# The same steps of an attention and gated-convolution kernel in another order on all five engines

## Chip, cores and metric

The kernel runs on one core of one Trainium2 chip. The metric is the device time of one execution in microseconds; the time given is the median of the runs.

## What is computed

The reference is block-sparse attention (4 batches, 8 heads, 768 tokens, head size 64) followed by a gated convolution layer. Cut to what matters:

```python
scores = scale * q @ k.T                       # per batch and head, 768 x 768
mask = neighbours | first and last block | 3 random blocks per query block   # blocks of 32
attn = softmax(where(mask, scores, -1e9)); x = attn @ v     # heads side by side: 4 x 768 x 512
h = maximum(x @ w_in, 0)                       # 512 -> 1024
conv_out = sum over k of conv_w[k] * h shifted by k - 1     # 3 taps along the tokens
out = (h * sigmoid(conv_out)) @ w_out          # 1024 -> 512
```

## The kernel before

The kernel first builds a graph of some 1,800 steps in Python. A step is a short run of instructions of one kind (two matmuls, one activation, one transfer), with the steps it depends on, the engines that can do it and the buffers that it takes. Which step comes when is not decided in the program: a long string, `ORDER`, gives the whole order. `put_down` reads it from left to right, two characters for a step, one more for its engine where there are several to choose from, one more for each buffer that the step takes:

```python
o = ops[64 * CODE.index(line[x]) + CODE.index(line[x + 1])]
x += 2
engines = list(o.alts)
e = engines[0]
if len(engines) > 1:
    e = ENGINES[line[x]]
    x += 1
for b in o.allocs:
    b.index = CODE.index(line[x])
    x += 1
if o.fn is not None:
    o.fn(e)
```

Each engine works through its own steps in the order of the string and waits, where a step needs it, for steps of other engines. PE, ACT, DVE, POOL and SP are each one list in order; a transfer that waits holds up what stands behind it in the list of its engine.

The work by stages, with the names used later and their lines in the profile:

- The head: q and k of the first pair of heads are loaded by SP and ACT and cast (`cast_q`, `cast_k`, L327 and L331), transposed on PE (`k_tr` L460, `q_tr` L500 and L522) and copied into a slot `t` of rows 0 to 63 (`k_cp`, `q_cp`). Rows 64 to 87 of the slot hold the mask, which DVE makes from the sampled blocks (`a1` to `a5`, L271 to L299, tile `mtok`) and which `m_k`, `m_q0`, `m_q1`, `m_h1`, `m_r1` and `m_slot` copy into the slots. So a matmul over 88 rows gives scores and mask at once. PE runs `warm` and `fill` matmuls on a zero tile (L230) until real work is there.
- Later pairs of heads are loaded by POOL (L239: `ld_k`, `ld_q`, `ld_nq`, `ld_v`), held back by small `pace` copies on POOL (L407, L673). From the seventh pair on, k and q are transposed by transfers of SP (`xb`, L597, tile `stg`) and copied by DVE (`stg_cp`). Mask rows of these slots come by SP (`m_turn`, `m_last`). v is copied by `v_cp`.
- Attention: 144 units of 8 blocks of 128 x 128 scores. Per unit two `s` steps on PE (L762, tile `st`, two buffers), one `exp` on ACT (L774, tile `pt`, six buffers; the first unit has two), two `av` steps on PE (L799, tile `av`, two buffers). Four pairs of heads end in `rcp` and `norm` on DVE (L707, L709, tile `xtok`), and the result is transposed, by SP (`x_xb`, L718) or on PE (`x_tr` L728 and a copy `x_cp`), into tile `xT`.
- The layer behind it runs by segments of 384 tokens (the last one as 256 and 128), while the attention of the next segment goes on: `f1` on PE (L896, tile `mix`, two buffers shared with transposes and outputs), `relu` on ACT (L916) or DVE (L918) into `hE`, then on DVE `mul` (L954) and `add` (L962), `tanh` on ACT (L1001), `g1` and `g2` on DVE (L1004, L1009) into `gT`. The very last segment makes the taps as matmuls (`conv`, L973) and its tanh at L978. `f2` on PE (L831) multiplies by the second matrix, `ev` on ACT (L327) or DVE (L331) copies to `o2s`, and `out` on SP (L840) stores it.

The tile `mix` is held by one step at a time, so `f1` of the next part waits for the `relu` of the part two before it. The two `st` buffers let PE be two units of scores ahead of `exp`.

Of the kernel before, what the change touches and what calls it, by code (L numbers as in the profile page):

```python
# [25 lines left out]
6y36g2016h6B16C6D46l1RV1QV2wV36m16G06H6u1s1n6v6z5Y06I51p4X1w4Y2X14Z1x4+2Z14/2+501y511z5234222V5ZV21V6n26P16Q6R0
6A6E6F6U06V6J6K1j6o6L06M6p06W16S06Z16+6T6N16qV6OV1r6/2720732e02fV2gV743ih16X77178iiik07f07g794il1q7k17l7h51i
ijV002KV47m0in16Y707p07q7r1imViF0iGiHiI71ioipV17u17v7w2iJiq0ir7C075762z1isViK2AV42BV7D7H17I7E32C07a7b17i7j7niN1
7c17J42s17M07N2tV7o7s7t7x537R17S2DV2uV2EViO147y7O57z2iP7AiQiz1iLiR7T03007W07X7Y17diAit082183iBA2842iu870887F17G
ivV37K7L2N18938c18d7PiM07Q7U7V2OV02PViw07e1iS312/18h0ixiyV8i7Z7+0852Q17/0iV2iW8e48j58p18q3823j38r0868a8b8f8u08v  # L30
2SViT80iYiX8w18g8k8l8z18A2RV7BiC08s18B28E08FiD8G3iU8J18K8L4iEVj918R08S8tja8x8T58y8C8D8W18H8X8I36254378/090iZi+
j13jf0jg8Y09112YV0j28m18nj4j333V32Vi/941958M8N08U8V8Z8+92939c09d962j5j01mj63919h19ijh979e498jbj7j89j5ji158O29m0
9n9r19sjc818ojjA09o1jdA13ajo0jp9w09t29909a35V18P3f3g33cV3bV553i3d0562F057jl1jmjnA9x9E19FjqV3eV2jJ08Q23k09y3ju0
jv9f09g9J0jKjM9K9G0jLjwVjN9k9l9p3h3o2T13p19q9L49O19Pjr19u2G09T09U9v9z2HV2IV9Q5jO9B19Cjs9/1jx09A19V2jyjzAa0a139D
9b3r3s0jtVjR1jSjP3w1jUjA1jBa402U0jCA3l9Ha5a91aaa619I9M9NjD1jEae09Raf9Sab42VV2WVaj1jFAjZ2jTjVjQj+ag53u3tjWak9W9X
jG0a20jH9Y2k09Zj/al0jIAar0a3a7a8kv13Dacasadaw1axjXjYkj0ahat3ay1aB0aiamaCan1auavkk3E13G3Ak1k53k6k7k8k9k29+k3k4
aD4kaaG1aHao1azaAkwaI5aO0aEaFaPklkx3B23F3M3N0aQ2aT1aUaV0kbkckmknV23nVapaJkyaY0aZb11b2aK3v43xkzA33qV33zV3yVa+3
b31kE0kFkB1kCb60b7aR0aS3H0aL0be1kDV14kGAkZ0k+k/l0kK0kLbfaWb84kMAbg5kH1kIbj0kJV53I1bkkQ0l1bl2kRkSAbo1kT13P3Q23S
kAjekobpaXbt0a/bub0b4l2bq03mVaMl51l6bv3kN0kOb5kUl8kPV6ld2bB1bCb9ba1bb2bD1kVA7kW0bG0bHbhkXbI4bibmbnbL1brl73R3XbM
bcbsbwbxbQ0bRaq03T0jkaNkYAbN5bS2kd1bd3JbE0bFkebV1bWkp0lelfl9lall3c10l3lg3CV4lhkqbJbKkrl41by1lbbObPbX0c2c61lic33  # L40
3UkfkgkhA3bzlmljlolnlplcc7c813OV0bAkslqlk3LVbTbUlz1bYcb0ccbZ1c4cg1lrls3KV3VV13WVcd4ktA1b+0b/c5c9cachci5lAlBcelC
lDA2co0cpct1cfculI0lF1lGlHVlJlKVm10cjm2m4cq0cv3cy0czm3m5cD1ckcEcA4cF53+3/343403Y141kilt1lL0cr0cl2cmcI0lMlNAcscJ
lulO0lPcwcQ1cK2cR4c4d0m6lQVm91mam7mbmcm8cS1lvlwcxcV0cWcBcCcG3ZV1c+1c/cHlxA0cX3d04lR0cL42494hd30d4c01441cN1mdcO
d50lSlU1cM1lTAlVdb1dccTcUmelWVmh2mimfdg0lX0dhl+1mklYl/dd5lZVdl1cYcZdi2d1dmd2d6d7de0m0Adn1cnmjmgku4i0dq0drd80mp3
d9mrmlmqmsmx0ds3lE4e4fdv1mtdwmD1dfdx4mmmElycP45dD0dEdI1djdkdF5dodpdtdJdudymydN0dadz1dGdHdOmnmudK24q4r1dP1dA2mo
mFmzdBmvmwdS1dT46V247VdU3mAmBV34a24gd+0d/mGdLe31dMdQe4mHV1e04e52dC24jmY0e80mV1e9mWdRed1dVeemZdW4v4n4s4tea04E4F2
mXV08m+VdX1nh0njdY4w1ei0n21n3ejm/0n0ef5e10eq1ere2e6e7ebdZmI4o0ek14Jn1A94bV2ev0n50ecewes4ninkn4Anlegehex2np1el
em1eA1eBeC0en0nq4kV3eonsepn6etn7Aaeun81n9eF0eGeN1eOnaAnx2eyezeDnb0nceH5eS0eEeTeInrnt4lVeP1eJne1eX1eYeQ0eK2eL4u
4m4xnyndAbeU4eZ2nmnunznfnAmJ0mKeRngVnF3nGnB4pV3f00eVeMmLf1f51eWf6nvnnnHno0f25mP1mQmMfd0fef71mNA2ff4nCnInwnJ4yV4
mRe+e/fi1mSfjf34zVnDmTA0fn0f4o30o4fk2o5Ao61foo7fs1ftfp54G4Bo8Vot0ounEov4C14H4I4PnKnL4Q2fu3nN0nOf8f91fa1nMnT1ow  # L50
fA0fBnUfgnPfF1nVmC4K0484LoxfbfC04DA4fGfH1oyfhnQnRV1fK0nWflfLnZ0fmnXV3n+fc04RV0oz4MV04NVo01o1fP1fM4fQfU0fqfrfvfV
fwn/Ao2AfR2oAol1omfx0onfW5oofyopfD0oc0g01g1g23o91fEodg50oeAg6g70oqfInSoafJobVoB2oDoCof0ga1fNgbfOgc1fSoggf0ggoi1
fTfXfY1ojg3g4g8orohAgh4okAgn1gog9gs0gtoEfZ2osoX0oYgdmOnYfzf+oFoJ3oLgp2oKoMoGmU4A4Ogx1geoHgu5gygigjgq0oR1oSgrgv
gwf/gG0gHgk1oNoIgz3gloOgL1gMgI0gN1gAoToZgBoPoQoUo+gQ0gC0oVV1gDgRgZ1p71g+gS4g/2p8p9pah20h3h71o/V2h45pbV3gmpd0pe
pg1phpfV1cpiVh8hg0pm0pnh93poApB0pDpj1pkhhhl1gE0plAdgJ1gKgOgPhmgFA1hi0oWp0hn1pp1ps0gTgUpqh00h1h5pCpEhq0h6ptpFpG
prAehahbhrpuApJ1pKhs4gV2gWpLpMhz1hj1hc1pNhdhAgX1gYVpHpR2hkpOpv0pwhohe1hE0hFhphthuhfApxAfpy1pzpI1pSp10p2hB2hG5
pAAhv0pThwpPhC0hN1hOhP3p3hDhx1pUpQpVpWhyVhW0hHhJ2p4p5A0qk1hI1qlpZ3hKp+p/qmAghXqq0qrh/1hY0qsAhq0pXq1qB0qDq2qR1pY
q3qChQqh1hRq4qihL0i0i80i9hMA2hZ0h+q50q6i11i2q7q8qjAiia4i41hS0i5qn1i30ibqt2hTicquqSq9A1qwid2qEi60qoi7AqpAjqb0qc
ieqFhU1hVAqvqGqdif1qJ3igAqxpcqHqeqfA2ri1rjrkAqyqKqIqLqMqzr90rarbArA1qUqArf1rBrC0qNrgrhArc0rl0rmrdrn2qgqap6reAqO
qTrorprDqPqVqQrv1rwr31rq0r4rrrs2rtrurx3qWryrzrErL0rR1rF0r5rMrGrHrNrOqXqYrIrSrTrUr6rJA3rPA2rKrVVrWrQr7A1r8qZ0q+  # L60
# [997 lines left out]
```

## Time and profile before

| | us |
|---|---|
| Median of 3 runs (lowest, highest) | 207.86 (207.11, 208.13) |
| Span of the profiled execution | 205.4 |
| Its own time beside the span | not recorded apart from the runs; the median lies 2.46 above the span |
| Busy: PE, ACT, DVE, POOL | 197.1, 189.7, 184.9, 59.4 |
| Weight loads on PE | 142.3 |

A busy time is the union of an engine's records. Matmuls are pipelined and their records overlap, so a busy PE says less than the pace at which matmuls follow each other; both are used below. A row of the groups gives line, engine, operation, tiles, shape and count, then busy time and mean length in ns, then the engine's idle time ahead of these instructions and what ended it. A row of the timeline or of the chain gives start and length in us, engine, line and count. A row of the windows gives for each engine the busy time in that stretch and the number of instructions, then the granted clock, the share of the transfer engines and GB/s.

### The profile page before, as it was taken

The page shows a single profiled execution, that of the slowest core. Times are in us where ns is not written, and L with a number is a line of the kernel's source. Part 1 is how long each engine was busy: PE and PEld are TensorE (multiplying, and loading weights), DVE is VectorE, ACT ScalarE, POOL GpSimd, SP SyncE. Part 2 cuts the span into 40 slices and gives each one's busy share as a digit, 9 for nine tenths or more (in the row PEclk, how much of TensorE's full clock was granted, in tenths as well). Part 3 has the DMA queues.
Part 4 walks back from the last instruction along what each step waited for, and adds up shares of the span by engine and source line. Part 5 has one row for each costly group of instructions (what it writes and reads, how often), then busy time and mean ns, then how long its engine had stood idle before and what let it go on. Part 6 is the DMA issues. An engine that isn't in the chain of part 4 may idle for free.

```text
span 205.4 us, 6237 instructions
## 1 busy us (share of the span) xinstructions
PE 197.1 (96%) x2392; PEld 142.3 (69%) x2409; DVE 184.9 (90%) x572; ACT 189.7 (92%) x253; POOL 59.4 (29%) x113
## 2 busy tenths in 40 slices
...
GB/s 155 196 190 154 186 178 114 197 127 88 154 150 126 125 103 138 218 166 163 95 105 226 97 117 123 175 154 126 14 174 88 21 123 51 3 2 3 153 3 204
DMA packets 50969, 25.59 MB, mean 125 GB/s; under 512 B 36764, under 2 KB 47996, under 8 KB 50940
## 3 DMA queue, kind: packets, MB, share of 16 engines
...
q10 hardware_dynamic: 288, 0.30, 0.5%
q14 instruction: 10, 0.08, 0.1%
...
## 4 chain that ended last, share of the span: by engine, by line
PE 68%; ACT 15%; DVE 12%; issue 3%; ACTq 0%; DVEq 0%
PE st L762 22%; PE mix L896 15%; PE mix L831 15%; PE av L799 12%; ACT pt L774 11%; DVE m L954 3%; DVE t L331 2%; DVE m L962 2%; ACT m L1001 1%; DVE xtok L709 1%; PE st L831 1%; ACT vt L327 1%; DVE diag L379 1%; ACT hE L916 1%; PE mix L728 1%
## 5 line engine op out<-in xcount | busy, mean ns | idle before, releaser
L774 ACT ACTIVATE pt<-st 128x1024 bf16<-128x1024 f32 (+1 forms) x145 | 142.2, 1051 | 4.2 <-PE st L762 3.7
L762 PE MATMUL st<-t 88*128 88x256 bf16 (+2 forms) x600 | 90.5, 267 | 2.3 <-DVE t L331 1.2
L799 PEld LDWEIGHTS <-pt 128*128 128x128 bf16 x1152 | 54.0, 97 | 14.2
L762 PEld LDWEIGHTS <-t 88*128 88x128 bf16 x600 | 48.9, 97 | 21.0 <-issue 1.9
L799 PE MATMUL av<-vt,pt 128*128 128x65 bf16 x1152 | 60.5, 193 | 0.1
L896 PE MATMUL mix<-xT,winb 128*128 128x384 bf16 (+2 forms) x288 | 55.2, 307 | 0.1
L954 DVE TENSOR_SCALAR m<-hE,cw 128x382 bf16<-128x382 bf16 (+2 forms) x192 | 49.1, 312 | 0.4 <-ACT hE L916 0.2
L831 PE MATMUL mix<-woutb,gT 128*128 128x512 bf16 x167 | 47.2, 379 | 0.7
L962 DVE TENSOR_TENSOR m<-m 128x764 bf16<-128x764 bf16 (+2 forms) x64 | 34.1, 532 | 0.6
L896 PEld LDWEIGHTS <-winb 128*128 128x128 bf16 x288 | 24.0, 97 | 9.2 <-issue 0.6
L1001 ACT ACTIVATE m<-m 128x764 bf16<-128x764 bf16 (+2 forms) x32 | 27.1, 853 | 0.0
L831 PEld LDWEIGHTS <-gT 128*128 128x128 bf16 x200 | 17.1, 97 | 10.0 <-DVE gT L1009 1.2
L407 POOL COPY pace<-pt 1x1 bf16<-1x1 bf16 x24 | 6.4, 268 | 54.1 <-ACT pt L774 54.0
L916 ACT ACTIVATE hE<-mix 128x384 bf16<-128x384 f32 (+2 forms) x39 | 19.8, 519 | 0.4 <-PE mix L896 0.2
L1009 DVE TENSOR_TENSOR gT<-m,hE 128x764 bf16<-128x764 bf16 (+3 forms) x36 | 18.2, 509 | 0.4
L709 DVE TENSOR_TENSOR xtok<-av,rcp 128x384 bf16<-128x384 f32 (+2 forms) x36 | 18.3, 507 | 0.4
L239 POOL DMA_DIRECT2D nat<-in_q_dram x23 | 17.3, 752 | 3.8 <-DMA nat<-in_k_dram 1.6
L918 DVE TENSOR_SCALAR hE<-mix 128x384 bf16<-128x384 f32 x25 | 13.7, 553 | 4.3 <-PE mix L896 3.7
L331 DVE COPY t<-mix 64x384 bf16<-64x384 bf16 (+1 forms) x33 | 13.2, 411 | 0.6 <-PE mix L460 0.2
L239 POOL DMA_DIRECT2D nat<-in_k_dram x15 | 12.0, 803 | 3.0 <-issue 2.4
L1004 DVE TENSOR_SCALAR m<-m 128x764 bf16<-128x764 bf16 (+3 forms) x36 | 11.9, 334 | 0.7 <-ACT m L1001 0.7
L327 ACT COPY o2s<-mix 128x512 f32<-128x512 f32 x15 | 9.2, 613 | 3.3 <-PE mix L831 3.2
...
## 6 DMA issues: line engine op xcount, KB each, us to landing
...
```

The costliest lines, as they stand in the source:

```text
L239: return op(name, {eng: occ}, lambda e: on(e).dma_start(out=dst(), in_=src), prio, deps, dma=(kind, service), **kw)
L709: nm = op("norm", {"DVE": t_dps(128 * C)}, lambda e: nc.vector.tensor_tensor(out=xtok_t[xk.index][:, 0:C].rearrange("p c h d -> p h c d"), ...
L762: nc.tensor.matmul(out=st[:, 128 * x:128 * (x + n_)], lhsT=t[0:88, 12 + 6 * hh + kc, :], rhs=t[0:88, idx:idx + (n_ - 1) * (2 if P < NPE el ...
L774: nc.scalar.activation(out=pt_t[ptb.index][:, c0:c1], in_=st_t[stb.index][:, c0:c1], func=AF.Exp, bias=0.0, scale=0.125)
L799: nc.tensor.matmul(out=o[:, off:off + 65], lhsT=pt_t[ptb.index][:, 128 * x:128 * x + 128], rhs=V_t[vslot_b[P].index][:, hh, kc, 0:65], sta ...
L831: nc.tensor.matmul(out=acc(), lhsT=gT_t[gb.index][:, ffc, 128 * t:128 * t + 128], rhs=woutb[:, ffc, c0:c1], start=(ffc == 0), stop=(ffc == ...
L896: nc.tensor.matmul(out=mix_t[hb.index][:, w1 * y:w1 * y + w1], lhsT=winb[:, fc, 128 * ffc:128 * ffc + 128], rhs=xT_t[xt_buf[n].index][:, f ...
L916: nc.scalar.activation(out=dst, in_=src, func=AF.Relu, bias=0.0, scale=0.5)
L954: nc.vector.tensor_scalar(out=m_t[cb.index][:, x, y, 0:w], in0=hE_t[heb.index][:, f0 + y, t0 + x:t0 + x + w], scalar1=cw[:, x, f0 + y:f0 + ...
L962: nc.vector.tensor_tensor(out=m[:, a_, :, 0:w], in0=m[:, a_, :, 0:w], in1=m[:, b_, :, 0:w], op=ALU.add)
L1001: th = [op("tanh", {"ACT": t_act(2 * w) + 0.04}, lambda e, cb=cb, w=w: nc.scalar.activation(out=m_t[cb.index][:, 0, :, 0:w], in_=m_t[cb.in ...
L1009: nc.vector.tensor_tensor(out=gT_t[gtb.index][:, f0:f0 + 2, t0:t1], in0=m_t[cb.index][:, 0, :, 0:w], in1=hE_t[heb.index][:, f0:f0 + 2, 1 + ...
```

## The change

The string `ORDER` is replaced. Nothing else in the program is changed; the new string has one line less, so every line of the changed kernel stands one lower in its profile (the exp at L773 instead of L774). All steps and their instructions are the same. Their order differs on all five engines, so do the buffer numbers, and 51 of the steps that ACT or DVE can do go to the other of the two. In sum `relu` goes from 39 on ACT and 25 on DVE to 31 and 33, `ev` from 16 and 9 to 14 and 11; in the head one `cast_q`, one `m_h1` and `m_r1` go from DVE to ACT, and of `k_cp` and `q_cp` as many go one way as the other. The order is the result of the same kind of search as before, with stretches of the clock and two transfer queues that share in what the search assumes, begun from the order before.

The first lines of the diff, cut:

```diff
 ORDER = """
-000211g010M030405060708090a0S0T1T01U230251262h12j20U0L0O0N0P0Q0R0b0c0d0e0f0g0h0i0j0k0W1e0V0X12V13A17V1AV30Y1CA
-1DA1f1d1E01K10l1H01FA00Z1LV10V0/A0m0n0o0p0q5805911JV1BV1h1GA1IA0r0s0t0u0v1M05a05b0w0x0y0z0A0B0C0D5e05f1NA0+16V
...
+0M0L0S00010210U0N0T0O031T1040P050W060Q071U0812A13V090R0a1O10V1e0b17A0c0d1f1g2311AV20e1CA0f0g0h0i0Y1DA2501E01K10Z
+0j1FA00k0l0m0n0o260p1H01LA0/V10A1GV1/31BA1i1JV1IA0q0r0s0t0u0v0w0x5800+5912d05a50y1M011V5b5e016V2x25f18A1NV0X5g0
...
```

Read out, the head's steps up to the second exp, on ACT and DVE:

```
before ACT  ld_q0 ld_k0 m_k cast_k cast_k k_cp m_q0 k_cp k_cp exp exp
after  ACT  ld_q0 ld_k0 m_k m_h1 cast_k cast_k k_cp q_cp m_q0 cast_q k_cp exp exp
before DVE  warm_mem v_one ident_mem a1 nblk v_one a3 ident24 m_k m_h1 cast_q a4 v_one v_one a5 q_cp m_q0 k_cp cast_q
after  DVE  warm_mem ident_mem a1 nblk m_k a3 v_one v_one v_one cast_q a4 a5 m_q0 k_cp he_zero k_cp a5 m_q1 m_h1 q_cp
```

More of the change, by code (lines that the diff above doesn't have):

```diff
@@ L20 @@
 ORDER = """
-000211g010M030405060708090a0S0T1T01U230251262h12j20U0L0O0N0P0Q0R0b0c0d0e0f0g0h0i0j0k0W1e0V0X12V13A17V1AV30Y1CA
-1DA1f1d1E01K10l1H01FA00Z1LV10V0/A0m0n0o0p0q5805911JV1BV1h1GA1IA0r0s0t0u0v1M05a05b0w0x0y0z0A0B0C0D5e05f1NA0+16V
-1SA05j11V15k0E5g15c05d1Y05l211V18V191WV11XV5o05p5q35h1k15i0F1+V1ZV5t15u0G5m0H5n5C05D1O02k1/12d22x31b1a2v21l24V1
-0I0J5r5v45s4S5E55H15I2702a15M05N5J05O10K5R15S5T25w5x15F5G28V22bV2cV29V5+05/5K5L5P6035y02iV21t5z1o631642l1654680
-692o05Q6d16e5U2mV32nV2pV2qV6a55V5A16i06j6f06106266671c5W12y5BV06r16s6k11u1P06b6c4T2r34U2J04V2L04W1v2M6t26w05X6x
@@ L26 @@
[L26 to L60, printed above, removed]
@@ L61 @@
-q/r0r1A0r2
+0M0L0S00010210U0N0T0O031T1040P050W060Q071U0812A13V090R0a1O10V1e0b17A0c0d1f1g2311AV20e1CA0f0g0h0i0Y1DA2501E01K10Z
+0j1FA00k0l0m0n0o260p1H01LA0/V10A1GV1/31BA1i1JV1IA0q0r0s0t0u0v0w0x5800+5912d05a50y1M011V5b5e016V2x25f18A1NV0X5g0
+5j1190z5k0A0B1V04S2h05l32j30C1Y11h1d1WV10D5o05p0E0F0G1XV1SA05t11+V5c00H1ZV2k5q11a5u0I5d5h1k12y0J5v25i5C00K1l1b5D
+5m5n5r5E05H14T24V32r25I1t5s2705J44U5M02J228V25N5w2a129V5O55x14V5F5R12bV5S5G2cV5T12iV25+05y05/1o2v05K5L5P1p1j600
+5Q6312L0645z5U2l06551u6802mV3692o15V4W2nV6a26102M6d16e2pV622qV5A01v6f366675BV16i06j1r4X6b1w6k46c1P16r12wV16s4Y
@@ new lines @@
+5W02KV42X16g2e06t56h6w01QV1RV6x4Z5X1x6l6y31m6B16C6m16n26D06u2011q6G06H2gV2fV6v6z6A6I45Y06P15ZV6Q6E22V21V6F6R16o
+6U06J6V4+6K2Z36p16W36L06S06Z16M6+6T6qV6/26N07206OV6X731c6Yik074477170781sih17957f07giiil7h1ijV0h7k17limV4/7175
+7m0767p0iF37a7q2s17c2iG7b17r37iin07d7u17viI2uA7e0io7w27C02tV7jiH7D7niq12+ipVj7E114iriJ7o502z01yisV7H1iK7s7I300
+2AV4517M01z7J47tiN07x7Niz1iOiA7O32BV7R17SiBV07y2C07T07F0iQ7z07G7W07XiL2N17Y2522DV7K3408212EV83iP7Lit08412OV0870
+882PV537P361iu8947A8c18divVg2Q12/17B7Q8e57U7V2SV8h0iR8iiw08j0iM07Z31ix7/18p17+185iS8qiyV808u0868a8r22RV8b8fiV38g
@@ new lines @@
+8viC0iW818w18k8z135V28AiT8liDiX8B58E0391iY8F8s08tiU8G08J1iZ8K8x8yiEV8C8L48R03f548m08S37j918T2j128n33V8W13g28Xjf0
+8D8Y1558o8H8I8/0j22YV38M32V90i+3d194195jg913563ij3j4jai/8N1j58U9608V8Z9c0j08+9d3a8O192j6938Pjh15979e5989h1j79i
+382992jbj89j29m01n8Q29nji9a9o0jcjjV29f19r19sjdV1jo03r2F39t3jp3cVjl13k09b573bVjm2T0jqA9w03eV0jnA9x3s39E19y49FjJ3
+ju13h9gjK9kjv9G1jL9J03o3p19KjM9l9pjr09q9L5jN3u9O1jsjwVjO9u9PjtV9v9z9T09Q09B19UjR02G19A09H2IVjA09V32HVjBjS9I9/1jP
+a0jCA9MjU3w13ta40a11jx1jTa53A9N3B02U0jVa649Rjy2VV3la912WV9S9WjWjzVaa9Xae09Cafab2jG1a21jD0jZ1jEag03Daj13E1ak9Y2a3
@@ new lines @@
+j/j+a7al3a8ar0jXasjFVacadahat4jH9Zaw1axjYjQaijIAaman0aB0k03Gay0auk50aCavkv1k7k1aD1kw3j3je9+azaG1k6k2aH9D3v4k8aA
+aO0aEaFaI5kj0aPk9kkk3kaao0k4aJaT1aU3xaQ1apkbaKkxklkcaV3aY0aZ3nVaR1aSkma+23mV3PaW3Q0aL2aXknV33I0kyb113FkzV0b2b60
+b30kE03MaMaq0b73yVkFkB1b85kCkAbe1kDV0hbfaNa/3Sbj0bg4kGV3N2bkkH13CV1kK0bl1kLkZ13qV4jk3H0bo1k+b0bpkMAb4k/b5bt0bq3
+kIl03JkQ0kRbul1kJA2b93zVl2ba0bhbB1kSV3T1bCkW1l3bD5bil50bmkN03OV3bnbv4bb1kXbrl41kObcbG1bHkYAl6kPVibL0bsbwbxby0bz
+bAbdbI1bMbE1bFkd0l8bN5bQ1l7bRkT1bS2kUl9bJbV0bWld3kVA5bKke3+lflebX13Rkp1c113/3bO3LVlac2bPbT3KVc60c35c7lbkqll1bUkf
@@ new lines @@
+lgc80bYlckgkrlh433Xcb0lmkhA2ksln3UbZ0lic4ccktV0locg1c5cd3c940cachlz0lp3Y0ci4440kilI1b+1ljlJceb/co0lqcplkcfkulA
+lKVcq3c02ct1lrcucjcklslF1cv2cy0cl03VV1lGkoczlHVlBcA4lCm13cD1m3cElDA1lO14c3WV4d1cF1lPlEm241cI0lR0lQVcJcQ1m4cK5cR
+cr1cslL1m5lMcS03ZV0cwcxlNVcBcV0cCcmm6cGcW4hc+1m90cnc/lt1lSm7d04m8lumbma4i1lTAcHd31cX1d442lU0mccLlVcM0494a2cN2cT
+cOcUlWAcYlvmd4ed55l+0mh1cZdb0midclwmemjdg1dd0dhlxV2d1d2l/d6mklydi1lX1mfd7dl0m0VdmlYmldn4dq1de1lZVdr45cPmD0ds2mp3
+4q4fdfdv0d81djmrdkdodwmmmq4r0dpmx1mgdx1dD1dEmsd9dtmEdadF0dudI0mtmydJmnmudydz0modN1dGdH4gdK2dOmvmFdA0mw4vmzdP14s
@@ new lines @@
+dS0dLdMmG4n4o0mAmHA0dTmBV3d+1dU0d/mV0dBmWmY1e034jmXV17mZe30e4m+AdQe81m/0e55dC0nh2n0nidRe9n1A4dV4E4tdWed04F2ea2
+4bV1dX1e11een2146V2e2ef1n8047Vei1dYnkej4w0n3ek44kV3eq0e6e7ern94un4VnjdZebev1es5np04Jecegewnrn51ex34GeheleA0eBen0
+naV4lVem04Bn64C1eC1eF1eteGnqeoeun7AaeyezeN0eH3nx1eDeO4xne1nfnb0nsnceP2eEnyndVd4HepeS1nlngAeTeX0eI4pV4eU4eYnF3mP1
+nteJeZ0mJ0eQ1eK2nHf01f1eRnAeLnueVeWeMf22nze+mQf50mRnG4Inmf6e/nvmCmKnB4K14P4Q2f70mLnn4yV4f3fd1feno0f4f8f90mMmIff3
+nIfi0fjmNA2mS4zVnJfn1fk4o30fa0mTV1o4nCfonwmUfs0fgo5VnN1fp5nDft4L4DV2nEfhfu0flo60o7fmo8VnOmOnKnPot04AfqnT0fA0ov
@@ new lines @@
+4RA0oufBfF1nLfC4fGowfrfvfwnMnUfH0nVoxnWfboynQfx1nXV3fK1fLnRA14MV0fP0fQfM2ozfD1o00nYfc24NVo148oAfR3nZ1n+fyfU1n/A
+fVo2V4O4mfzfEfIfJg00fW1g1ol3omo90oc1g25ong51g6ooodoag74fNopfOfSoeVga0oqgbobVgf1of1gc2fToB1ogggoroi0ohAoDojgh0oC
+fXfY0gn0osg3g4okAg8oEg9gogdoJ0gs1gp4gtgeoKoR0fZ0gu1gioFoX1gx0gyoGoMoLoYf+gG1gHgz3gjoNoSf/oHgq1groOgk2gvoIgwgL0gM
+nSgI5gAoPoToQgBoZgN3glgQ1oUgC1gmgDgJ0gKoVA0gOo+gRo/A2gZ0oWg+gPp70g/1p8p9gS3papd1pbA1peh20pfA1dpg0phh3piVgE1h71
+h44gTgFV1pB3h8gUh01pm0h92pDpnpj1gV1pCpkpoAgWhg0plA0hhpEhl1hi5pJ2hmh1h5h6pKhahbps1hn4pLhq0hrhc2pFpp0hs1pthdpMpq
```

5 lines of the change are left out of this document (added).

## Prediction

> **What bounds the kernel now.** I read the page first, then the windows, then the chain in order of time. Times are microseconds.
>
> ```profile
> span 205.4 us, 6237 instructions
> PE 197.1 (96%) x2392; PEld 142.3 (69%) x2409; DVE 184.9 (90%) x572; ACT 189.7 (92%) x253; POOL 59.4 (29%) x113
> PE 68%; ACT 15%; DVE 12%; issue 3%; ACTq 0%; DVEq 0%
> ```
>
> Three engines are over 90% busy and the chain that ended last runs mostly over PE. The median of the runs, 207.86, is 2.46 above this span. The change touches nothing in what lies around the span, so I work in differences of the span and add them to 207.86.
>
> How full is PE really? Its records overlap, so I take the pace at which matmuls follow each other from the chain in order of time (start, length, engine, line, count), and the numbers of matmuls from the page's groups.
>
> ```profile
> 78.27 0.87 PE st L762 x8
> 79.27 1.30 PE mix L896 x8
> 172.25 0.48 PE av L799 x16
> 187.96 0.44 PE mix L896 x4
> 193.13 0.45 PE mix L896 x8
> 199.59 2.17 PE mix L831 x10
> 201.79 0.58 ACT o2s L327
> ...
> L774 ACT ACTIVATE pt<-st 128x1024 bf16<-128x1024 f32 (+1 forms) x145 | 142.2, 1051 | 4.2 <-PE st L762 3.7
> L799 PE MATMUL av<-vt,pt 128*128 128x65 bf16 x1152 | 60.5, 193 | 0.1
> L896 PE MATMUL mix<-xT,winb 128*128 128x384 bf16 (+2 forms) x288 | 55.2, 307 | 0.1
> L831 PE MATMUL mix<-woutb,gT 128*128 128x512 bf16 x167 | 47.2, 379 | 0.7
> ```
>
> A unit of scores (1024 columns) takes 0.435 (the 8 matmuls in 0.87 are two units), so 144 units take 62.6. The 1152 av matmuls at 0.48/16 = 0.030 take 34.6. Of the 288 first-layer matmuls the code makes 224 of 384 columns (1.30/8 each: 36.4), 32 of 256 (0.11 each: 3.5) and 32 of 128 (0.45/8 each: 1.8), together 41.7. The second layer is 184 matmuls of 512 columns at 0.217 (39.9; the page shows 167, records are missing) and 16 of half that (1.8), together 41.7. The 99 transposes, 24 convolution matmuls and 26 fills that come after the first real work have 128 or 130 columns each: 149 at 0.056, 8.3. The sum is 188.9. PE begins real work at 4.26 (a row further down) and ends its last matmul at 199.59 + 2.17 = 201.76, which is 197.5. So all of PE's waiting is 8.6. No order can win more than that, and the 3.6 behind the last matmul (last copy and last output) are the same steps in both orders, on ACT and SP.
>
> Here the Trainium skill would judge otherwise: its page "Perfetto Trace Analysis" (section Identifying the Most-Contended Engine) holds that the busy share of matmuls says little of PE's headroom and that the busy share of weight loads tells it. By that the 69% of weight loads would leave 63 us. This case's spacing does not bear that out: the waits that the pace leaves room for are 8.6.
>
> ACT and DVE stand behind PE, stage by stage (window, PE, PEld, DVE, ACT, POOL busy, clock, DMA):
>
> ```profile
> 40.00:60.00 20.00, 19.84 (x262) 14.35 (x263) 19.22 (x57) 20.00 (x25) 8.24 (x16) 1.00 0.93 131
> 60.00:80.00 20.00, 19.75 (x255) 14.12 (x256) 18.42 (x53) 19.98 (x27) 5.75 (x12) 1.00 1.00 126
> 100.00:120.00 20.00, 19.84 (x246) 14.19 (x247) 18.76 (x57) 19.59 (x26) 6.60 (x13) 1.00 0.82 133
> 120.00:140.00 20.00, 19.95 (x229) 13.80 (x228) 17.59 (x52) 19.18 (x25) 7.95 (x14) 1.00 1.24 149
> 140.00:160.00 20.00, 19.81 (x222) 13.54 (x223) 19.36 (x56) 19.73 (x28) 0.00 (x0) 1.00 0.41 90
> ```
>
> Up to 100 ACT has no free time; DVE has 0.6 to 2.4 free in each 20. The granted clock is 1.00 throughout.
>
> **What the change does, part by part.** Instructions and their sizes are the same. What differs is the place of nearly every step in its engine's list (on PE by 4 steps on average, on ACT by 4, on DVE by 6, on POOL by 1, on SP by 2), some buffer numbers, and the engine of steps that ACT or DVE can do.
>
> *The engines' load.* Counted from both order strings, relu goes from 39 on ACT and 25 on DVE to 31 and 33, and the output copy (ev) from 16 and 9 to 14 and 11.
>
> ```profile
> L916 ACT ACTIVATE hE<-mix 128x384 bf16<-128x384 f32 x31 | 15.8, 524 | 0.1
> L918 DVE TENSOR_SCALAR hE<-mix 128x384 bf16<-128x384 f32 x25 | 13.7, 553 | 4.3 <-PE mix L896 3.7 <-ACT pt L774 0.5
> L327 ACT COPY o2s<-mix 128x512 f32<-128x512 f32 x15 | 9.2, 613 | 3.3 <-PE mix L831 3.2
> L331 DVE COPY o2s<-mix 128x512 f32<-128x512 f32 x8 | 5.5, 690 | 2.9 <-PE mix L831 2.9
> ```
>
> ACT loses 8 x 0.52 + 2 x 0.61 = 5.4, DVE gains 8 x 0.55 + 2 x 0.69 = 5.8. Three small steps of the head go the other way (about 1 on ACT, below). ACT comes to about 185, DVE to about 190: the loads change places, and both stay under PE. The shift comes early and is partly taken back: ahead of the 96th exp ACT has 4 relu and 5 ev less, ahead of the 132nd 8 and 4, after it 2 ev return.
>
> *The head.* The rows up to the first exp:
>
> ```profile
> 2.91 0.32 DVE L289 CAST ident<-ident 24x24 f32<-24x24 bf16 x1
> 2.97 0.70 ACT L327 COPY t<-nblk 24x384 bf16<-24x384 bf16 x1
> 3.69 1.07 ACT L327 CAST nat<-o2s 128x384 bf16<-128x384 f32 x2
> 3.83 0.35 DVE L331 COPY t<-t 24x768 bf16<-24x768 bf16 x1
> 4.26 0.34 PE L460 MATMUL mix<-ident,nat 128*128 128x128 bf16 x3
> 5.57 0.61 DVE L299 SCALAR_TENSOR_TENSOR mtok<-sbi,keyid,A 24x384 bf16<-24x384 int32 x1
> 6.21 0.40 ACT L327 COPY t<-mtok 24x256 bf16<-24x256 bf16 x1 [1.08 <-DVE mtok L299]
> 6.64 0.47 ACT L327 COPY t<-mix 64x384 bf16<-64x384 bf16 x1
> 7.01 0.60 PE L762 MATMUL st<-t 88*128 88x384 bf16 x4 [1.25 <-DVE t L331]
> 7.67 1.07 ACT L774 ACTIVATE pt<-st 128x512 bf16<-128x512 f32 x2
> ```
>
> The first scores wait for the mask rows, which ACT could copy only at 6.21, after DVE's mtok. The new order puts the ident24 cast (0.32) behind the head and the mask copy of 24x768 (0.35 on DVE) on ACT, and puts two vt memsets of under 0.1 in: mtok starts near 5.0. ACT pays: the 24x768 copy is not in ACT's rows; from 0.35 (DVE's) to 1.4 (twice the 24x384 row) I take 0.7. Its casts then end at 5.5 instead of 4.8, the k copy (0.47) and the first q copy (0.47, formerly DVE's) at 6.4, with the last mask column behind them, so the scores start near 6.5, and the first exp, behind one more cast and copy, near 7.15: 0.5 earlier. At 1.4 for the copy this is gone.
>
> *The stretch from 10 to 160.* Of the 8.6 of waiting about 1.45 is the head's (1.25 in the row of 7.01, the rest before the q transposes), some 7 lies in small pieces. Up to 100 they go with an ACT that has no gap; relieving ACT by 4 x 0.52 + 5 x 0.61 = 5.1 ahead of the 96th exp must let some go. What is late next is PE itself. Between 0 and half of the 7 I take 1.0: the pure exps before 30 cannot be relieved, and each moved step adds a DVE step on a full DVE.
>
> *Transposes and loads.* SP's and POOL's lists are reordered too. The closest transposes of xT before, with their first use:
>
> ```profile
> DMA to landing us min/median/max: 2.4/3.8/6.1
> ...
> 136.90 1.19 SPq L718 DMA_TRANSPOSE xT<-xtok  x1
> ...
> 141.83 1.14 PE L896 MATMUL mix<-xT,winb 128*128 128x384 bf16 x6
> ```
>
> That is 4.9 from issue to use. In the new order the work put between the last transpose of a segment and its first f1 is, for the same segment, 6 f2 pairs, 7 half units and 6 av quads: 6 x 0.434 + 7 x 0.218 + 6 x 0.12 = 4.8; for the segment before it 4.7, for the last full one 3.3, for the other three 5.6 to 9.0. A median landing (3.8) fits all but the 3.3; that one lies behind POOL's last load, with few transfers beside it, and I take the minimum of 2.4 for it. I price this part at nothing, with 0 to 2.7 as its bounds (rival below).
>
> *POOL's loads under a fuller DVE.*
>
> ```profile
> L239 POOL DMA_DIRECT2D nat<-in_k_dram x15 | 12.0, 803 | 3.0 <-issue 2.4
> ```
>
> An issue takes 0.80 beside a DVE that is 90% busy, and POOL is 29% busy, so 5 more of DVE costs nothing here. The Trainium skill's page "SBUF — State Buffer" (section SBUF: two separate sides, the box on DVE blocking DMA) warns that a software-issued load starves while DVE holds the shared port, some 3.1 instead of 0.62. By it each of the loads would be over 2 late; the row of 0.80 does not show it, so the sum is without it.
>
> Sum: 0.5 + 1.0 = 1.5 off, 205.4 to 203.9 in the span, 207.86 to 206.3.
>
> **Rivals.** *Nothing moves* (0.28): PE already follows itself at full pace, and the waits, being of dependences rather than of load, come back elsewhere; only the head's half remains, or less: 207.4. For it: 8.6 in 197.5 is little. Against it: ACT's full windows.
>
> *DVE becomes the bound* (0.17, slower). By the 132nd exp, near 160, DVE has 8 relu and 4 ev more: 8 x 0.55 + 4 x 0.69 = 7.2. In the five windows above it was free for 0.78 + 1.58 + 1.24 + 2.41 + 0.64 = 6.65, much of it waits for PE's f1 (3.7 in L918's row). It decides from the point where under 5 of that can be used; if half can, DVE is 7.2 - 3.3 = 3.9 late, the gates and f2 with it, less the head's 0.5 and 1.0 of pieces: 207.86 + 2.4 = 210.3. For it: the chain's 12% on DVE; against it: muls and adds have slack until f2 needs them.
>
> *Transposes land late* (0.10, slower): if the two at 4.7 and 4.8 land at 6.1, PE, which takes its list in order, stands still for 1.4 + 1.3 = 2.7: 206.3 + 2.7 = 209.0. It decides at landings over 4.7.
>
> *ACT was the whole reason* (0.08): half of the 7 goes, with the head 0.5 + 3.5 = 4.0: 203.9.
>
> **How the numbers follow.** The forecast has 0.37. I count 0.5%, 1.04 here, as what a measurement tells from no change. Faster are the forecast and the last rival, 0.45; same is the first, 0.28; slower are DVE and transposes, 0.27. The range from 204.2 to 210.3 leaves out most of the last rival and the part of DVE's above its price, about 0.15. The likeliest case's own range is 205.4 (2 of the 7) to 207.3 (no head).
>
> **What would show it.** Right: first exp before 7.3; ACT near 185 and DVE near 190 busy, last matmul end 1 to 2 earlier than 201.76; the windows from 40 to 100 reach the same exp earlier. Wrong: PE's idle time put down to DVE gT, DVE stg copies or to DMA xT; DVE at 20.0 of 20 from 100 to 160 with ACT waiting for st; a new wait of over 1 in front of an f1.

## The result: 2.9% slower

| | before | after |
|---|---|---|
| Median of 4 runs (lowest, highest), us | 207.63 (207.11, 208.13) | 213.58 (212.78, 214.37) |
| Ratio, 95% interval | | 1.0286 (1.0249 to 1.0323) |
| Span of the profiled execution, us | 205.4 | 211.0 |
| Its own time, us | not recorded apart | 212.78 |

The forecast was 206.3, with a range up to 210.3; the time lies 3.3 above the range. The medians are 5.9 apart, the spans of the two profiled executions 5.6. Where some executions of a kernel in this document fell into a slower state of the chip, its time is the median of the others. The page of the changed kernel has these lines:

```profile
span 211.0 us, 6165 instructions
...
PE 198.6 (94%) x2390; PEld 142.7 (68%) x2409; DVE 188.8 (89%) x579; ACT 190.3 (90%) x246; POOL 64.2 (30%) x113
...
PE 46%; DVE 37%; ACT 10%; issue 5%; ACTq 0%; DVEq 0%
```

No engine has become busier than PE. What is new is the chain that ended last: its share on DVE went from 12% to 37%, and PE's from 68% to 46%. The windows (same columns as above):

```profile
40.00:60.00 20.00, 19.31 (x249) 13.84 (x249) 19.67 (x58) 19.16 (x22) 6.80 (x12) 1.00 0.91 123
60.00:80.00 20.00, 19.20 (x251) 13.66 (x250) 19.72 (x57) 18.93 (x25) 8.64 (x14) 1.00 0.97 140
...
100.00:120.00 20.00, 18.46 (x205) 12.40 (x205) 19.07 (x52) 17.34 (x22) 7.07 (x12) 1.00 0.95 154
120.00:140.00 20.00, 19.89 (x251) 14.30 (x252) 17.05 (x50) 19.30 (x25) 11.10 (x20) 1.00 0.91 115
140.00:160.00 20.00, 19.18 (x196) 12.52 (x198) 19.39 (x57) 18.66 (x23) 0.00 (x0) 1.00 0.67 122
```

From 40 to 80 DVE and ACT have changed roles, as the forecast said: ACT, which had no idle time there, now has 0.8 to 1.1 in each 20, and DVE, which had 0.8 to 1.6, has 0.3. But PE, which had 0.2 idle in each of these two windows, has 0.7 and 0.8, and from 100 to 120 it has 1.5. The granted clock is 1.00 in all of them, as before, so it plays no part there.

The starts of the same exp in both traces show where the time went. The table gives the lag of the changed kernel behind the kernel before, in us:

| exp | 1st | 7th | 25th | 31st | 49th | 55th | 79th | 85th | 91st | 103rd | 121st | 145th |
|---|---|---|---|---|---|---|---|---|---|---|---|---|
| lag | -0.38 | 0.16 | 0.63 | 1.35 | 1.38 | 2.82 | 1.81 | 3.37 | 4.60 | 6.10 | 6.34 | 5.69 |

The head's gain is gone by the seventh exp. The rest is lost in three stretches, and hardly anything after the 103rd exp. The shares of the chain by line from 84 to 102, the 70th to the 81st exp, say who sets the pace there (the lag is 1.9 at the 70th exp, 1.2 at the 80th and 3.9 at the 81st). The second line is the kernel before, from 80 to 98, where it has the same exps:

```profile
by line: DVE m L953 32.3%; DVE m L961 14.0%; DVE t L330 10.4%; DVE hE L917 9.2%; issue 8.1%; DVE xtok L708 5.7%; ACT pt L773 5.6%; DVE m L1003 3.5%; DVE o2s L330 3.4%; DVE vt L330 3.3%; DVE gT L1008 2.8%; PE mix L895 2.8%; DVE rcp L706 2.1%
...
by line: PE st L762 32.9%; PE mix L896 25.4%; PE mix L831 21.0%; PE av L799 20.6%; issue 0.6%
```

In the changed kernel it is nearly all steps of DVE, one behind the other: the taps' products (L953) and sums (L961), among them the copies of the slots (t) that PE needs. In the kernel before it is PE alone.

### The profile page after: what moved, and what is told of

Its sections match the earlier page's. It is cut to its first block, busy times and chain, and to the rows that moved or that the text cites. A ratio compares the mean times of both kernels' runs of the same rounds, so it can differ in the third digit from the quotient of the medians.

```text
span 211.0 us, 6165 instructions
## 1 busy us (share of the span) xinstructions
PE 198.6 (94%) x2390; PEld 142.7 (68%) x2409; DVE 188.8 (89%) x579; ACT 190.3 (90%) x246; POOL 64.2 (30%) x113
## 4 chain that ended last, share of the span: by engine, by line
PE 46%; DVE 37%; ACT 10%; issue 5%; ACTq 0%; DVEq 0%
PE st L761 13%; PE mix L830 12%; PE mix L895 12%; DVE t L330 10%; DVE m L953 9%; PE av L798 7%; ACT pt L773 6%; DVE m L961 4%; DVE hE L917 4%; DVE xtok L708 3%; ACT t L326 2%; DVE diag L378 1%; DVE gT L1008 1%; DVE vt L330 1%; DVE o2s L330 1%
## 5 line engine op out<-in xcount | busy, mean ns | idle before, releaser
L773 ACT ACTIVATE pt<-st 128x1024 bf16<-128x1024 f32 (+1 forms) x145 | 140.6, 1022 | 8.3 <-PE st L761 5.7
L798 PEld LDWEIGHTS <-pt 128*128 128x128 bf16 x1152 | 56.3, 97 | 16.8 <-ACT pt L773 2.0
L798 PE MATMUL av<-vt,pt 128*128 128x65 bf16 x1152 | 63.7, 193 | 1.6 <-ACT pt L773 0.9
L761 PEld LDWEIGHTS <-t 88*128 88x128 bf16 x600 | 47.7, 97 | 20.1 <-DVE t L330 1.5
L953 DVE TENSOR_SCALAR m<-hE,cw 128x382 bf16<-128x382 bf16 (+2 forms) x192 | 49.8, 315 | 0.6 <-ACT hE L915 0.3
L961 DVE TENSOR_TENSOR m<-m 128x764 bf16<-128x764 bf16 (+2 forms) x64 | 33.8, 532 | 0.4
L406 POOL COPY pace<-pt 1x1 bf16<-1x1 bf16 x24 | 11.0, 457 | 54.3 <-ACT pt L773 54.1
L917 DVE TENSOR_SCALAR hE<-mix 128x384 bf16<-128x384 f32 x33 | 17.8, 551 | 6.9 <-PE mix L895 6.2
L830 PEld LDWEIGHTS <-gT 128*128 128x128 bf16 x200 | 16.9, 97 | 10.1 <-DVE gT L1008 1.3
L238 POOL DMA_DIRECT2D nat<-in_q_dram x23 | 18.4, 801 | 2.5 <-issue 1.9
L915 ACT ACTIVATE hE<-mix 128x384 bf16<-128x384 f32 (+2 forms) x31 | 15.3, 501 | 0.4 <-PE mix L895 0.3
L1003 DVE TENSOR_SCALAR m<-m 128x764 bf16<-128x764 bf16 (+3 forms) x36 | 11.8, 329 | 0.8 <-ACT m L1000 0.4
L330 DVE COPY t<-stg 64x1536 bf16<-64x1536 bf16 x20 | 12.0, 601 | 0.3
```

The lines of the kernel that those rows point to most:

```text
L238: return op(name, {eng: occ}, lambda e: on(e).dma_start(out=dst(), in_=src), prio, deps, dma=(kind, service), **kw)
L330: nc.vector.tensor_copy(out=dst, in_=src)
L761: nc.tensor.matmul(out=st[:, 128 * x:128 * (x + n_)], lhsT=t[0:88, 12 + 6 * hh + kc, :], rhs=t[0:88, idx:idx + (n_ - 1) * (2 if P < NPE el ...
L773: nc.scalar.activation(out=pt_t[ptb.index][:, c0:c1], in_=st_t[stb.index][:, c0:c1], func=AF.Exp, bias=0.0, scale=0.125)
L798: nc.tensor.matmul(out=o[:, off:off + 65], lhsT=pt_t[ptb.index][:, 128 * x:128 * x + 128], rhs=V_t[vslot_b[P].index][:, hh, kc, 0:65], sta ...
L830: nc.tensor.matmul(out=acc(), lhsT=gT_t[gb.index][:, ffc, 128 * t:128 * t + 128], rhs=woutb[:, ffc, c0:c1], start=(ffc == 0), stop=(ffc == ...
```

## The experiments

Each run stands against the kernel before. "Order" means the order string, rewritten so that each step still comes behind those it needs; lines in the traces of the experiments are those of the kernel before.

### The engines of relu and ev, one way and the other

```diff
 e1: changed order; relu 31/33 -> 39/25 and ev 14/11 -> 16/9 on ACT/DVE; every place stays
 e2: order before;  relu 39/25 -> 31/33 and ev 16/9 -> 14/11; every place stays
```

> The changed order, with every relu and output copy on the engine it had before (ACT and DVE loads of these as before: DVE 5.8 less, ACT 5.4 more than in the change). Theory A, the moved relu and ev steps fill DVE and it holds PE up: most of the 5.9 loss goes, under 209.7. Rival B, the places of the steps in the lists are the cause and not the load: 212 or more, since ACT gets the work back in an order not made for it.

> The order before, with every relu and output copy on the engine that the change gave it. Theory A: DVE is now too full in this order as well, 210.5 or more. Rival B: within 1 of 207.6.

Measured: 215.05 (ratio 1.0360, 1.0315 to 1.0404) and 224.39 (1.0803, 1.0757 to 1.0850). Giving the work back to ACT does not return the time, and moving it to DVE in the order before costs 16.9. So places and engines fit each other: the changed order costs 5.9 with its own engines, and 7.6 with those of the kernel before. Read from the order strings, each of the two runs moves 34 steps, 22 one way and 12 the other, of which the net is the ten that the forecast counted. With this the effect of the load alone cannot be told from that of the places.

### Room on DVE

```diff
-            lambda e, cb=cb, w=w: nc.vector.tensor_scalar(
-                out=m_t[cb.index][:, 0, :, 0:w], in0=m_t[cb.index][:, 0, :, 0:w], scalar1=1.0, ...
+            None
```

> The changed kernel without the 36 g1 instructions of DVE (11.8 busy in its profile); this leaves out the addition of 1 to the tanh. Theory A: with DVE relieved by twice what the change put on it, the time falls by 5 or more, to 208.5 or less. Rival B (waits are places in the lists, transfers or PE itself): it falls by under 2.5, to 211 or more.

> The kernel before without the same 36 g1 instructions. Theory A, where DVE had room before: it falls by 2 or less, to 205.6 or more, since PE's pace leaves 8.6 of waiting in all. Rival B: it falls by as much as the changed kernel does.

Measured: 211.03 for the changed order (1.0151, 1.0111 to 1.0190) and 207.21 for the order before (1.0005, 0.9985 to 1.0024). What was left out, g1, is this row of the changed kernel:

```profile
L1003 DVE TENSOR_SCALAR m<-m 128x764 bf16<-128x764 bf16 (+3 forms) x36 | 11.8, 329 | 0.8 <-ACT m L1000 0.4
```

11.8 less on DVE gain about 2.5 in the changed order and, within the interval, nothing in the order before. So DVE's work does lie on the path of the changed kernel for about 2.5, and did not before. That is at the edge of the rival (211 or more) and far from the 208.5 that a full DVE as the cause would have given: without g1 the two orders are still 3.8 apart, so most of the loss is not DVE's load.

### The transfers' lists

```diff
 e5: changed order on PE, ACT, DVE;  SP and POOL in the order before
 e6: order before on PE, ACT, DVE;   SP and POOL in the changed order
 e10: order before;                  only POOL in the changed order
 e11: order before;                  only SP in the changed order
```

> The changed order on PE, ACT and DVE, with the lists of SP and POOL (all transfers) in the order before. Theory C, the transfers' new places make transposes and loads land late and PE waits through DVE: 2 or more of the 5.9 loss goes, 211.5 or less, and the jump of 1.4 between the 48th and the 54th exp with it. Theory B, the compute lists alone: within 1 of 213.6 or above.

> The order before on PE, ACT and DVE, with the lists of SP and POOL in the changed order. Theory C: 209.5 or more. Theory B: within 1 of 207.5.

> The kernel before with GpSimd's list alone in the order of the changed kernel (the paced loads); SP's list (transposes and stores) and the three engines stay. Both lists together made the kernel before 5.3 us slower (212.96 us), with two stops in its trace: VectorE waited 1.35 us for a transpose into stg at 50.95 us, and ScalarE 2.84 us for a store of o2s at 109.1 us. Theory 'loads come late': the first stop comes from loads that are paced later and returns here, 208.8 to 209.3; the second does not. Rival 'stores and transposes stand in the wrong order on SP': within 0.6 of 207.6 here. Rival 'both lists are needed': within 0.6 here and in the run of SP's list.

> The kernel before with SP's list alone (transposes, stores) in the order of the changed kernel; GpSimd's list and the three engines stay. Theory 'a store queued behind transposes holds an o2s buffer': ScalarE's stop of 2.8 us for the store comes back, 210.2 to 211.5. Theory 'loads come late' alone: within 0.6 of 207.6. If the stop of VectorE at 51 us comes back here as well, 212 to 213.

Measured: 217.27 (1.0466, 1.0439 to 1.0493), 212.52 (1.0258, 1.0217 to 1.0299), 209.56 (1.0105, 1.0049 to 1.0161) and 215.24 (1.0325, 1.0240 to 1.0409). Each list costs time alone, SP's no less than both together. In the trace with both (e6), the lag is flat but for two jumps, and both have a row. First DVE's timeline, then ACT's and PE's, then SP's (start, length):

```profile
50.62 0.84 DVE L954 TENSOR_SCALAR m<-hE,cw 128x382 bf16<-128x382 bf16 x2
52.52 1.12 DVE L331 COPY t<-stg 64x1536 bf16<-64x1536 bf16 x2 [1.06 <-DMA stg<-nat]
...
108.09 1.02 ACT L774 ACTIVATE pt<-st 128x1024 bf16<-128x1024 f32 x1
111.95 0.59 ACT L327 COPY o2s<-mix 128x512 f32<-128x512 f32 x1 [2.84 <-DMA out_dram<-o2s]
...
113.51 0.60 PE L762 MATMUL st<-t 88*128 88x256 bf16 x4 [2.72 <-ACT pt L774]
...
106.33 1.03 SPq L840 DMA_DIRECT2D out_dram<-o2s  x2
108.03 1.24 SPq L718 DMA_TRANSPOSE xT<-xtok  x1
109.99 1.21 SPq L597 DMA_TRANSPOSE stg<-nat  x1
112.56 0.33 SPq L840 DMA_DIRECT2D out_dram<-o2s  x1
```

At 52.5 the copy of a slot waits for its transpose. At 109.1 ACT's next step is an output copy, whose buffer o2s (one of four) is still being stored; the last stores ahead of it were issued from 106.33 on, the copy could start at 111.95, and two transposes were issued in between. The next exp stands behind that copy in ACT's list although its scores are ready, and PE waits for the exp: a late store stops the matmuls for 2.7. Both stops come back with SP's list alone (e11), in its waits:

```profile
DVE t L331 <- DMA stg<-nat: 3.1, 2, 2.7
...
ACT o2s L327 <- DMA out_dram<-o2s: 2.0, 1, 2.0
```

So the first is SP's doing and not, as was expected with e10, POOL's; in the trace of e10 neither of the two stands at its place. In the changed kernel itself no wait for a store or for these transposes is named, and its order on PE, ACT and DVE with the earlier transfers is slower still (e5). So the new lists of SP and POOL suit the new lists of the three engines better than the earlier ones would, and neither pair of lists has a price by itself.

### The lead of the attention products

```diff
 e7: changed order, each av two places later in PE's list where it can be
 e8: order before,  each av two places earlier in PE's list where it can be
```

> The changed order with each av step two places later in PE's list and nothing else moved, so that scores run 4.0 units ahead of av on average (3.4 in the change, 4.1 before). Theory B, PE's list leaves too little between exp and av: 2 or more of the loss goes, 211.5 or less. Theory C: within 1 of 213.6.

> The order before with each av step two places earlier in PE's list and nothing else moved, so that scores run 3.4 units ahead of av, as in the change. Theory B: 209.5 or more. Theory C: within 1 of 207.5.

Measured: 223.53 (1.0755, 1.0717 to 1.0793) and 217.89 (1.0509, 1.0474 to 1.0543). Two places on PE cost about 10 in either direction. A longer lead alone does not return the time of the changed kernel; but the moved places have a price of their own, so these two runs do not tell what the lead is worth.

### A one-element copy that holds an exp

This is the widest single stop of the changed kernel in the stretch where it loses most, in its timeline:

```profile
98.39 3.11 POOL L406 COPY pace<-pt 1x1 bf16<-1x1 bf16 x2 [1.99 <-ACT pt L773]
...
99.39 1.00 DVE L953 TENSOR_SCALAR m<-hE,cw 128x382 bf16<-128x382 bf16 x4
...
101.53 1.94 ACT L773 ACTIVATE pt<-st 128x1024 bf16<-128x1024 f32 x2 [1.19 <-PE mix L895]
...
102.61 0.30 PE L798 MATMUL av<-vt,pt 128*128 128x65 bf16 x4 [0.76 <-ACT pt L773]
```

The row of ACT names a matmul of PE as the releaser, but what ended 0.03 ahead of the exp is POOL's second pace copy, at 98.39 + 3.11 = 101.50. That copy reads one element of an exp that had ended at 87.66; it stood in POOL's list behind another pace copy, and the exp that is to overwrite its buffer waited.

```diff
-    NSLOT, NSTG, NNAT, NNQ, NVN, NPT, NXK, NXT, NHE, NCV, NGT, NOS = 5, 2, 4, 4, 3, 6, 3, 3, 2, 4, 2, 4
+    NSLOT, NSTG, NNAT, NNQ, NVN, NPT, NXK, NXT, NHE, NCV, NGT, NOS = 5, 2, 4, 4, 3, 8, 3, 3, 2, 4, 2, 4
 (and the pt numbers in the changed order given out in turn)
```

> The changed kernel with eight buffers for the exponentials (pt) instead of six, given out in turn, so that the buffer longest free is taken; every list stays as it is. In the trace of the changed kernel three exponentials (the 53rd, 69th and 81st) start 0.24, 0.20 and 0.03 us after GpSimd's one-element pace copy has read the buffer that they overwrite, the last of them after ACT stood still for 1.19 us and PE for 0.92 us; eleven more start within 0.32 us of the end of the attention product that read theirs. Theory 'late pace copies hold the pt buffers': 213.6 us goes down by 1.5 to 3.0, to 210.6 to 212.1, and no exponential starts within 0.3 us after a pace copy of its buffer. Rival 'the waits only stand in front of other waits of the same length': within 0.8 of 213.6.

Measured: 213.88 (1.0305, 1.0270 to 1.0340); the theory fell. In its trace no exp starts within 0.3 of the end of a pace copy or an attention product on its buffer, so these waits are gone, and the time is the same. At the 55th exp the lag is 2.78 (2.82 without the edit), so the wait at the 53rd had stood ahead of another. Later a different one takes the place, in PE's timeline:

```profile
129.23 0.48 PE L896 MATMUL mix<-xT,winb 128*128 128x384 bf16 x2 [1.13 <-DMA xT<-xtok]
```

Here a transpose of xT is late, as in the prediction's rival of late transposes; in the changed kernel itself no matmul waited for one.

### Stretches and halves

```diff
 e12: order before up to the 78th exp, changed order from there
 e15: changed order up to the 78th exp, order before from there
 e13: changed order; steps between the 43rd and the 61st exp among themselves as in the order before
 e14: the same between the 79th and the 106th exp
```

> The lists of the kernel before up to its 78th exponential of 144, from there the changed kernel's. In the traces the changed kernel is 1.81 us behind at that exponential and 5.69 us behind at the last one. Theory 'each loss is made where it shows, by the lists of that stretch': the part after it remains, 3.9 us, so 211.0 to 212.0. Rival 'the losses come from how the early order loads the queues and buffers of the later': 207.4 to 209. Rival 'the parts don't fit where they are joined': over 213.

> The lists of the changed kernel up to its 78th exponential, from there those of the kernel before: the counterpart of the run with the second half alone, which took 1.4 us more than the kernel before. Theory 'the losses add up by halves': 207.6 plus the 1.8 to 3 us by which PE's waits in the first half grew, 209.4 to 210.6, and the two halves' losses come to 3.2 to 4.4 of 5.9 us. Rival 'the first half spoils the second, whatever its order': 212 to 213.6. Rival 'the parts do not fit at the joint': over 213.6.

> The changed kernel, in which only the instructions between its 43rd and its 61st exponential (50 to 75 us) are put in the order that they have among themselves in the kernel before; what stands in that stretch, the engines and all the rest stay. In this stretch the wait of PE for vector work (gT 0.73 us, t 0.91 us) set in. Theory 'the order inside the stretch makes the loss': about 1.4 us come back, 211.6 to 212.6, and the lag behind the kernel before stays near 1.3 us at the 55th exponential (2.82 us in the changed kernel). Rival 'what the stretch gets from the one ahead makes the loss': 213 to 214. Rival 'the order fits neither end': over 214.5.

> The same for the instructions between the 79th and the 106th exponential (96 to 134 us), the stretch in which the changed kernel falls behind by 4.3 us. Theory 'the order inside the stretch makes the loss': 2.4 us (PE's waits there beyond those of the kernel before) to 4 us come back, 209.5 to 211.5. Rival 'what the stretch gets from the ones ahead makes the loss' (its half cost 1.4 us after the first half of the kernel before): 212.5 to 214.5. Rival 'the order fits neither end': over 214.5.

Measured: 208.77 (1.0061, 1.0038 to 1.0084), 214.18 (1.0318, 1.0301 to 1.0336), 217.07 (1.0473, 1.0447 to 1.0499) and 219.30 (1.0578, 1.0544 to 1.0611). The second half alone costs 1.4, not the 3.9 that the traces show for it; the first half alone costs 6.8. By the medians the two come to 8.2, more than the whole change. Putting back the order inside the two stretches in which the time is lost does not return it but costs 3.5 and 5.7 more. The last three times are those of the rivals by which the parts do not fit where they are joined (over 213.6, and over 214.5): in the trace of the first half alone the lag goes from 4.0 to 5.6 right at the joint, between the 78th and the 79th exp. So these runs do not tell what the order of a stretch costs by itself; how each stretch fits what stands ahead of it and behind it matters at least as much.

### The head alone

```diff
 e16: changed order up to the second exp, order before from there
```

> The lists of the changed kernel up to its second exponential, from there those of the kernel before: its head alone, in which the first exponential began 0.38 us earlier. Theory 'the head is worth what the profile shows': 207.1 to 207.4, 0.1 to 0.2% under the kernel before. Rival 'the next waits take it back': 207.4 to 207.9.

Measured: 207.62 (1.0002, 0.9983 to 1.0020). The first exp starts at 7.31 instead of 7.67, and at the seventh the kernel is 0.19 late. ACT's timeline shows who took it back:

```profile
9.32 0.83 ACT L327 CAST vt<-m 128x768 bf16<-128x768 f32 x1 [0.58 <-DMA m<-in_v_dram]
10.06 4.67 ACT L774 ACTIVATE pt<-st 128x1024 bf16<-128x1024 f32 x5
```

ACT is there sooner, and the first load of v is not: the cast waits 0.58 for it, the next five exps stand behind the cast, and start at 10.06 (9.87 in the kernel before). This was the only part of the change that cost no time by itself, and it gained none.

### Moves with no aim

```diff
 e17: order before, 201 pairs of neighbours in DVE's list changed over
 e18: order before, 125 pairs of neighbours in ACT's list changed over
```

> The kernel before with 201 pairs of neighbours in VectorE's list changed over (every pair, from the front, that can be without a step standing ahead of one that it needs); the other lists stay. The change moved VectorE's steps by 3.6 places in the mean, these moves by 0.9. Theory 'each place in a list is fitted to when its data are there, also on an engine with idle time': over 212.6 us, 5 us or more slower, in many waits under 1 us. Rival 'VectorE, idle for 20 of 205 us, takes up moves of one place': 207 to 208.5. Were it so, the loss of the changed kernel would not come from its order on VectorE.

> The same in ScalarE's list: 125 pairs changed over, 0.98 places in the mean (the change: 0.55 among the steps that stayed on it). Theory 'each place is fitted': over 212.6 us. Rival 'PE's two st buffers and the six pt buffers take up one place': 207 to 208.5.

Measured: 223.20 (1.0747, 1.0697 to 1.0796) and 305.94 (1.4748, 1.4621 to 1.4874). Moving nearly every step of ACT by one place costs almost half the run. These are from the waits of that kernel (us in total, times, longest):

```profile
ACT pt L774 <- PE st L762: 66.2, 53, 3.0
PE st L762 <- ACT pt L774: 62.2, 54, 2.1
```

In that list 40 neighbouring exps have changed places. The one whose scores come later then goes first, and the scores behind it need the buffer of the one that waits: PE and ACT take turns, 1.2 a time. In this trace the granted clock of PE is also 0.50 from 20 to 40, so a part of the price there is the clock's. On DVE there is no such knot, and idle time of 20; a mean move of 0.9 places costs 16 all the same. These are from the waits of that kernel:

```profile
ACT pt L774 <- PE st L762: 13.4, 17, 2.4
PEld L831 <- DVE gT L1009: 6.4, 8, 1.7
```

Against 16 for moves with no aim, the change, which moved the steps that stayed on DVE by 3.6 places among themselves and PE's by 3.7, lost 5.9: it is a good order of its own, and not as good as the one that it was begun from.

## Why the prediction was wrong

**The head (forecast at 0.5 less): right in its steps, wrong in its worth.** The steps are all in the trace of the changed kernel:

```profile
3.68 0.83 ACT L326 COPY t<-t 24x768 bf16<-24x768 bf16 x1
...
4.53 0.93 ACT L326 CAST nat<-o2s 128x384 bf16<-128x384 f32 x2
4.59 0.61 DVE L298 SCALAR_TENSOR_TENSOR mtok<-sbi,keyid,A 24x384 bf16<-24x384 int32 x1
...
5.09 0.34 PE L459 MATMUL mix<-ident,nat 128*128 128x128 bf16 x3 [0.91 <-ACT nat L326]
...
6.69 0.60 PE L761 MATMUL st<-t 88*128 88x384 bf16 x4
...
7.29 1.07 ACT L773 ACTIVATE pt<-st 128x512 bf16<-128x512 f32 x2
```

The copy taken at 0.7 is 0.83, the casts end at 5.46 (5.5), the scores start at 6.69 (6.5), the first exp at 7.29 (7.15). The step that failed is the one after it: the 0.38 by which the first exp is earlier was counted as gain at the end without asking what is late next. With the head alone it was the load of v. In the changed kernel it was not: there the cast of v stands behind the fourth exp and waits for nothing, ACT has no gap over 0.2 from the first exp to the seventh, and by the seventh the lead is gone all the same.

The traces of the other runs show a second thing that the head's price left out. Nine of them have this head on PE, ACT and DVE. In five (e3, e5, e7, e13, e15) PE works at half its pace until between 10 and 11, and the first exp comes 0.9 later than in the kernel before, not 0.38 sooner. In e15, for one, the first scores and the first exp stand in PE's and ACT's timelines like this:

```profile
7.91 1.06 PE L762 MATMUL st<-t 88*128 88x384 bf16 x4
...
8.58 0.60 ACT L774 ACTIVATE pt<-st 128x512 bf16<-128x512 f32 x1 [0.41 <-PE st L762]
```

The same four matmuls take 1.06 instead of 0.60, and fills of 128 columns follow each other at 0.107 instead of 0.056, though the granted clock reads 1.00 in both. In the ten traces with PE's head of the kernel before, that kernel's own among them, PE has its full pace by the first scores each time. How often the changed kernel itself begins so is not shown: the only one of its four executions with a trace, the one above, is the fastest (212.78).

**The load: right on DVE, misread on ACT.** The moved work shows in the groups (after):

```profile
L915 ACT ACTIVATE hE<-mix 128x384 bf16<-128x384 f32 (+2 forms) x31 | 15.3, 501 | 0.4 <-PE mix L895 0.3
L326 ACT COPY o2s<-mix 128x512 f32<-128x512 f32 x13 | 7.7, 589 | 4.8 <-PE mix L830 4.8
...
L917 DVE TENSOR_SCALAR hE<-mix 128x384 bf16<-128x384 f32 x33 | 17.8, 551 | 6.9 <-PE mix L895 6.2 <-ACT pt L773 0.7
```

The 15 groups of ACT add up to 209.0 before, the 16 after to 201.8, 7.2 less, where 5.4 less about 1 was foreseen; 1.6 of it is in the row of the exps, which are the same in number (142.2 and 140.6). DVE was foreseen near 190 and is 188.8. But ACT's busy time rose from 189.7 to 190.3 instead of falling to 185. It is a union, and records of neighbours on ACT overlap: 209.0 - 189.7 = 19.3 of overlap before, 201.8 - 190.3 = 11.5 after, where ACT stops more often. A full ACT looked shorter than its work. The forecast took a difference of rows from a union; that is the mis-sized term.

**The stretch from 10 to 160 (forecast at 1.0 less): wrong in sign; this is the step that failed.** All the waiting of PE was put at 8.6, and I held that relieving ACT "must let some go". PE's real work now begins at 5.09 (the fence above) and ends with this piece of the chain, at 205.65 + 1.74 = 207.39:

```profile
205.65 1.74 PE mix L830 x8
```

That is 202.3 for the same 188.9 of paced work: 13.4 of waiting, 4.8 more, and 0.8 of later start. Two of the changed kernel's waits:

```profile
DVE hE L917 <- PE mix L895: 6.2, 4, 4.7
ACT pt L773 <- PE st L761: 5.7, 13, 1.0
```

ACT now waits 5.7 for scores instead of 3.7, since PE is late; DVE's longest wait, 4.7 for a first-layer matmul, lies behind the losses, from 171 on. As I read it now, ACT's full windows were no sign that ACT bound PE: an engine that is fed without a gap is full too. The sentence "What is late next is PE itself" failed: next was, for about 2.5, DVE (by the runs without g1). What the rest is late for stays open.

**Transposes at nothing: right for xT, incomplete as a step.** No wait of PE for a transpose of xT is in the changed kernel's trace, so the rival of late transposes did not come about there. But the step costed the transposes of xT alone, by the work on PE. The transposes into stg and the stores of o2s, which SP's new list moves too, had no price, and they are what stopped the kernel before under that list (2.7 and 2.0 in its waits, 1.0325 in its ratio).

**DVE as the bound (0.17): the right engine, another mechanism.** DVE is not at 20 of 20 from 100 to 160 (19.07, 17.05, 19.39), and the 7.2 of added work do not end as lateness there. The lag is 3.9 by 101.5 and 6.1 by 131, and 5.7 at the end. It came by place more than by load: returning the moved steps without the places did not help, and 11.8 less on DVE, twice what the change put there, gained 2.5.

**POOL's loads: right.** The 0.80 of an issue stayed under the fuller DVE (after):

```profile
L238 POOL DMA_DIRECT2D nat<-in_q_dram x23 | 18.4, 801 | 2.5 <-issue 1.9
```

Left out was what POOL's list does to ACT through the pace copies; it was there and, as the run with eight buffers showed, not what decides.

What stays open: of the 5.9, about 2.5 go when DVE has 11.8 less to do. For the other 3.4 no single place was found. The pt buffers, the transfer lists, the lead of av and the order inside the two worst stretches were each put back or relieved alone, and none returned time; each of these edits also moved or renumbered steps that fitted their neighbours, so none is cleared for good. The new buffer numbers (404 steps take other ones) and the new order of PE or of DVE by itself were not put back alone. That it is the sum of many waits under 1, each from a step that stands a place or two off, fits the moves with no aim, but is argued and not shown.
